# A second searched issue order for a fused attention and wave mixing kernel on one core

## The chip, the cores and the metric

The kernel runs on one core of a Trainium2 chip. The metric is device time in microseconds, the median of several executions; lower is better. TensorE (PE) multiplies matrices, VectorE (DVE), ScalarE (ACT) and GpSimd (POOL) work element by element, and SyncE (SP) only issues transfers. ACT and POOL issue transfers too. Each engine takes its own instructions strictly in the order in which they were written, and waits for the others by semaphores.

## The reference

Two blocks follow one another. All inputs are float32 in shape, with B = 4 batches, H = 4 heads, S = 1088 positions, D = 32 and R = 8.

```python
a = np.einsum('rd,bhsd->bhsr', S1, x)
b = np.einsum('rd,bhsd->bhsr', S2, x)
phi(x) = np.einsum('bhsi,bhsj->bhsij', a, b).reshape(..., 64)
...
kv = np.einsum('bhsf,bhsd->bhfd', phi(k), v)
z = np.sum(phi(k), axis=2)
num = np.einsum('bhsf,bhfd->bhsd', phi(q), kv)
den = np.einsum('bhsf,bhf->bhs', phi(q), z)[..., None] + 1e-06
x = (num / den), laid out as (4, 1088, 128)
...
theta = x @ w_theta
zr, zi = x * np.cos(theta), x * np.sin(theta)
y = einsum('ts,bsd->btd', w_tok_r, zr) + einsum('ts,bsd->btd', w_tok_i, zi)
u = x + y
return u + np.maximum(u @ w_ch, 0.0)
```

The two 1088 x 1088 token weights are the bulk of the arithmetic and of the loads. They arrive as 64-bit words and are decoded to float32 on the chip.

## The kernel before, in words

The kernel first writes its work down as a list of 1022 numbered operations (`Layout.op`), each with its engine (P for PE, V for DVE, A for ACT, G for POOL, S for SP), a function that issues its instructions, and the buffers that it reads and writes. The numbers follow the order of the program text. Then three tables decide the schedule, and nothing else does:

- `ORDER` holds the 1022 numbers in the order in which the operations are issued. An engine's own sequence is the part of `ORDER` that belongs to it, so moving a number moves the instructions and transfers of that operation past others on its queue.
- `PLACES` gives each of 419 buffers its slot in a pool: 22 slots of `big` (1152 words a partition), 5 of `zs`, one of `lv`, 6 of `hf`, 5 of `g3`, 6 of `g1`, 13 of `sm`, and 8 banks `ps` of the matmul accumulator. A buffer waits for the last reader of the buffer that had its slot.
- `SPINS` names operations ahead of which filler matmuls are issued ("70:2" is two ahead of operation 70). A filler (`spin`, L379) multiplies zeros, 128x384 in bf16, into a buffer that nothing reads. Ten more open the program and one stands after the first batch's scales.

In this order the operations' numbers are looked up when issued:

```python
self.order = [self.ops[int(i)] for i in ORDER.split()]
...
for o in self.order:
    n, home = spins.get(o.i, 0), None
    ...
    o.fn()
```

The stages of the work, batch by batch, are these.

- **Loads.** k, q and v of each batch are single transfers of 576 KB on SP (L614), batch 3's q four transfers (L609). w2 holds the two 128 x 128 weights of the second block. The token weights come in 17 rows of 1088 KB (L583, `zs` slots); ACT turns the two halves of each word into a float and a step (L584, L586), DVE shifts and adds them (L309 and the custom operation at L305).
- **Keys.** Transposes on PE, the features, and kv (`kfeatures`), the gram sums for the scales (`key_sums`), and a long chain of small DVE and PE operations that yields scales in powers of two (`chain`): once for batch 0, once for batch 1, and once for batches 2 and 3 together. The third starts with a sum over partitions: a DVE reduction (L849) and a matmul with ones (operation 281).
- **Queries.** Slices of q at fixed scale (`query_slices`), matmuls that give the feature sums at several precisions (`levels`, three PE operations a batch; ACT copies them out at L1002), and the denominator on DVE (L1003 to L1033, stage "den", which begins with the rounding that the profile shows as L309 `big<-lv`).
- **x, theta and z.** For each of three groups of columns: an outer product on DVE, its transposes (on PE for batches 0 and 1 at L1064, and for batches 2 and 3 by `turned`), the numerator on PE, theta on PE, two sines on ACT (L1114 to L1117 with the copies at L1111), and z = x cos, x sin on DVE (L305 `zs<-ps,g` or `zs<-g,g`).
- **turned** (L322): DVE transposes 32 x 32 blocks (L326); SP and ACT each scatter half of the result to DRAM in two transfers (L333, `fq` for outer products and `fx` for x); SP reads it back in the wanted layout (L338).
- **Mixing.** Batches 0 and 1 multiply each of the 17 z blocks by the matching weight row (`mix_row`), batch 0 for all three spans of columns (384, 384, 320) at once, batch 1 span by span. A float32 matmul shows as two records in the trace, so a row of batch 0 has six records and a step of batch 1 two. Batches 2 and 3 share seven products after Winograd (`winograd`), with sums of weight blocks on DVE (stage "ac").
- **Output.** The sum x + y, a matmul with w_ch, relu, sum and a transpose (`finish`, `finish_turned`), then stores of 32 columns each on SP and ACT (L1215).

The order of the stages in `ORDER` around the change: batch 1's mixing runs on PE while the queries of batches 2 and 3 go through DVE, ACT and the transfers. The first Winograd product follows as soon as batch 2's first z block is there.

Transfers issued by SP and ACT share a set of eight semaphores that are taken in turn, the "shared transfer queue of eight places": a transfer can be issued when the one eight before it has landed.

Of the kernel before, what the change touches and what calls it, by code (L numbers as in the profile page):

```python
# [76 lines left out]
)  # L77
SPINS = (
    "70:2 15:3 137:1 211:1 424:2 128:1 168:1 174:2 176:1 521:2 "
)  # L80
WARM = 0
SPLIT = ()
# [1330 lines left out]
```

## Time and profile before

| what | value |
|---|---|
| median of 3 runs | 219.65 us (219.24 to 219.75) |
| span of the profiled execution | 217.4 us |
| median less span | 2.25 us |
| instructions in the profile | 5063 |
| POOL and ACT, busy share | 10%, 51% |
| HBM read and written | 30.43 MB, 5.18 MB |

The profiled execution has no other time of its own than its span, which runs from its first to its last instruction. Times are microseconds. In the timeline views a row has the start, the duration, the engine, the source line, the operation, the tile that it writes, the tile that it reads, the shape, and how many alike follow one another; in brackets stands the idle time of the engine before it and what ended it. In the chain of waits a row has the start, the duration, the engine, the tile and the line. In the table of transfers the last column is the median time from issue to landing. An "x4" behind a matmul counts records.

### The profile page before, as it was taken

Reading aid. Unit: us, or ns where it says so; the run is one execution under the profiler, and the core shown is the slowest. Engines: PE = TensorE matmul, PEld = TensorE weight load, DVE = VectorE, ACT = ScalarE, POOL = GpSimd, SP = SyncE. Lnnn points to the kernel's source line nnn. Section 1 sums busy time; section 2 is a strip of 40 time slices with the busy share of each in tenths; the row PEclk is TensorE's granted clock in tenths of the full one; section 3 lists DMA queues with packets and bytes.
Section 4 is the critical chain, followed back from the end, with each engine's and each line's share of the span. In section 5 each row is a group of like instructions: output and inputs, shape, how many; then the busy total and the mean of one; then the engine's idle time right before and its main releaser. Section 6 shows DMA issues by size and latency. Waiting matters only on the chain.

```text
span 217.4 us, 5063 instructions
## 1 busy us (share of the span) xinstructions
PE 209.3 (96%) x1998; PEld 154.3 (71%) x1998; DVE 181.2 (83%) x408; ACT 111.2 (51%) x214; POOL 22.2 (10%) x44
## 2 busy tenths in 40 slices
PE   7999899999999999999999999999999999999994
PEld 3987786686766686666766575667758788888883
DVE  4899999999999999999599839988138999996542
ACT  3998498899779999983322040354037400000010
POOL 2237000055000000100132000100101000000000
PEclk9999999999999999999999999999999999999998
DMA  5999996869979979894226998599911000045253
GB/s 153 429 406 340 425 399 203 333 224 271 267 276 361 361 264 380 219 198 126 33 36 102 222 137 199 105 156 151 231 78 32 0 0 0 3 66 89 36 79 75
DMA packets 52635, 40.58 MB, mean 187 GB/s; under 512 B 45444, under 2 KB 47108, under 8 KB 50436
## 3 DMA queue, kind: packets, MB, share of 16 engines
q1 hardware_dynamic: 35540, 33.71, 48.7%
q0 software_dynamic: 1728, 4.65, 10.5%
q10 hardware_dynamic: 15344, 1.90, 6.0%
q8 instruction: 15, 0.25, 0.5%
q14 instruction: 8, 0.07, 0.1%
HBM read 30.43 MB, written 5.18 MB: 164 GB/s over the span
## 4 chain that ended last, share of the span: by engine, by line
PE 72%; DVE 12%; ACT 8%; DMA 4%; ACTq 2%; issue 2%; SPq 1%
PE ps L341 66%; DMA big<-q_l 2%; DVE lv L305 2%; PE ps L1064 2%; ACTq L333 2%; PE ps L1098 1%; DMA fx<-g 1%; DVE g L305 1%; DVE big L305 1%; PE ps L967 1%; ACT big L584 1%; ACT big L937 1%; DVE hf L309 1%; DVE zs L305 1%; ACT g L1068 1%
## 5 line engine op out<-in xcount | busy, mean ns | idle before, releaser
L341 PE MATMUL ps<-big,zs 128*128 128x384 f32 (+4 forms) x398 | 109.7, 424 | 0.4 <-DVE zs L305 0.4
L341 PEld LDWEIGHTS ps<-big,zs 128*128 128x128 f32 x398 | 71.4, 190 | 30.3 <-issue 2.6
L1201 ACT COPY g<-ps 128x128 f32<-128x128 f32 (+1 forms) x3 | 0.9, 301 | 42.5 <-PE ps L1193 42.5
L305 DVE CUSTOM_DVE_ANT_0 big<-big,big 128x2176 uint16<-128x2176 uint16 x17 | 21.8, 1287 | 0.4 <-ACT big L586 0.2
L584 ACT ACTIVATE big<-zs 128x1088 f32<-128x1088 f32 x17 | 20.9, 1235 | 2.1 <-DMA zs<-w_tok 1.2
L586 ACT ACTIVATE big<-zs 128x1088 int32<-128x1088 uint32 (+1 forms) x18 | 21.3, 1184 | 0.1
L341 PE MATMUL ps<-big,big 128*64 128x64 f32 (+2 forms) x208 | 20.6, 276 | 0.0
L341 PEld LDWEIGHTS ps<-big,big 128*64 128x64 f32 (+1 forms) x208 | 16.5, 154 | 2.9 <-issue 0.2
L305 DVE TENSOR_TENSOR big<-big,big 128x544 f32<-128x544 f32 x24 | 16.7, 712 | 0.0
L1002 ACT COPY lv<-ps 128x480 f32<-128x480 f32 x12 | 6.3, 563 | 14.2 <-PE ps L341 14.2
L312 DVE SCALAR_TENSOR_TENSOR g<-g,ps 128x384 f32<-128x384 f32 x12 | 6.6, 548 | 8.1 <-ACT g L1111 8.1
L1078 ACT COPY big<-ps 128x384 f32<-128x384 f32 x12 | 5.9, 489 | 14.0 <-PE ps L341 8.3
L309 DVE TENSOR_SCALAR big<-big 128x1088 int32<-128x1088 int32 x17 | 12.2, 724 | 0.6 <-ACT big L584 0.5
L341 PEld LDWEIGHTS ps<-w,big 128*128 128x128 f32 x80 | 10.6, 192 | 2.3 <-ACT g L1068 0.6
L319 POOL DMA_DIRECT2D big<-hf x6 | 5.4, 957 | 63.3 <-DVE g L312 33.8
L319 POOL DMA_DIRECT2D g<-big x6 | 5.2, 920 | 64.8 <-ACT g L1179 34.7
L341 PE MATMUL ps<-w,big 128*128 128x128 f32 x80 | 11.8, 280 | 0.0
L305 DVE TENSOR_TENSOR g<-lv 128x768 f32<-128x768 f32 x12 | 11.2, 945 | 0.0
L341 PE MATMUL ps<-g,sm 128*64 128x384 f32 x48 | 10.1, 507 | 0.2 <-ACT big L1078 0.2
L305 DVE TENSOR_TENSOR zs<-ps,g 128x768 f32<-128x768 f32 (+2 forms) x15 | 9.4, 632 | 1.0 <-PE ps L1098 0.9
L341 PEld LDWEIGHTS <-hf 128*64 128x64 f16 (+1 forms) x288 | 7.7, 110 | 2.9 <-issue 1.7
L379 PE MATMUL ps<-idle 128*128 128x384 bf16 x27 | 7.8, 400 | 1.3 <-POOL idle L381 1.3
(194 smaller groups left out, 336.6 us busy)
## 6 DMA issues: line engine op xcount, KB each, us to landing
zs<-w_tok SPq DMA_DIRECT2D x17, 1088.0 KB, 7.0
big<-k_l SPq DMA_DIRECT2D x6, 576.0 KB, 6.6
big<-hf POOLq DMA_DIRECT2D x6, 576.0 KB, 6.0
big<-v_l SPq DMA_DIRECT2D x4, 576.0 KB, 7.0
g<-fq SPq DMA_DIRECT2D x6, 384.0 KB, 5.2
big<-q_l SPq DMA_DIRECT2D x3, 576.0 KB, 5.1
fq<-g SPq DMA_DIRECT2D x12, 96.0 KB, 4.0
fq<-g ACTq DMA_DIRECT2D x12, 96.0 KB, 4.1
```

What stands on the lines that cost most here:

```text
L305: eng.tensor_tensor(out=o, in0=a, in1=b, op=f)
L309: (eng or V).tensor_scalar(out=o, in0=a, scalar1=s1, scalar2=s2, op0=op0, **kw)
L312: (eng or V).scalar_tensor_tensor(out=o, in0=a, scalar=s, in1=b, op0=op0, op1=op1)
L319: op("G", 0.9, lambda: G.dma_start(dst(), src(), accum_op=ALU.add), w, r, fly=fly)
L333: E.dma_start(there().rearrange("(a i) (x b j) -> b i x a j", a=nf, b=nf, j=SQ)[f], blocks()[f * SQ:(f + 1) * SQ].rearrange("i (x a j) -> ...
L341: T.matmul(o, lhs, rhs, start=start, stop=stop, skip_group_check=True)
L379: T.matmul(nowhere() if home is None else view(home, (GW,), F32), idle()[:, 0:P], idle(), start=True, stop=True, skip_group_check=True)
L584: op("A", 0.22 + n * 0.0009, lambda: A.activation(dfn(), words_of(raw(), n)[1].bitcast(F32), AF.Prelu, scale=2.0**-112, alpha=-(2.0**32)), ...
L586: op("A", 0.22 + n * 0.0009, lambda: A.activation(stp(), words_of(raw(), n)[0].bitcast(U32), AF.Copy, scale=2.0**-29), [stp], [raw])
L1002: op("A", act(480), lambda g=g, lp=lp: A.copy(lv().rearrange("p l (c n) -> p l c n", n=HR)[:, :, g * GC:(g + 1) * GC], lp().rearrange("p c ...
L1064: T.transpose(tr()[:, i * P:(i + 1) * P], qp()[:, i * H + 2 * n:i * H + 2 * n + 2].rearrange("p h i j -> p (h i j)"), ident())
L1078: op("A", act(GW), lambda g=g, xp=xp: A.copy(xt()[:, g * GW:(g + 1) * GW], xp()), cells(xt, g * GW, (g + 1) * GW), [xp])
```

## The change

Only the three tables are changed. No operation is added, removed or altered; the same 1022 numbers stand in `ORDER` in another sequence, so line numbers behind the tables fall by two. Positions that are the same on an engine's own list: 21 of 358 on PE, 33 of 347 on DVE, 27 of 214 on ACT, 8 of 38 on POOL, 17 of 66 on SP. 375 of the 419 places differ. There are 16 fillers by the old `SPINS` and 9 by the new, beside the ten and the one that stay.

```diff
 ORDER = (
-    "6 4 2 5 44 0 1 45 50 3 47 7 340 8 48 46 11 9 10 49 12 29 58 13 30 70 83 84 64 76 71 14 77 85 96 15 88 72 89 78 "
...
+    "6 4 0 5 44 1 58 47 45 7 50 8 340 9 49 10 11 2 48 12 29 355 84 83 70 30 76 13 46 71 64 85 14 59 86 88 77 15 61 87 60 "
...
 )
 SPINS = (
-    "70:2 15:3 137:1 211:1 424:2 128:1 168:1 174:2 176:1 521:2 "
+    "70:2 160:1 95:1 105:1 111:2 174:1 176:1 "
 )
```

Where the moved pieces that matter below stand, by operation number. Loads on SP, in their order:

```
before: s_t k0 q0 q1 k1 row1 k2 v0 k3 w2 row2 row5 row4 v1 ...
after:  s_t k0 w2 k1 q0 q1 row1 k3 k2 row4 v0 row2 v1 row0 row5 ...
```

Around operation 281 (batches 2 and 3's scale chain): operation 494 (a row of batch 0's mixing), 579 to 583 and 625 to 629 (steps of batch 1's mixing), 406 to 409 (row 14's decoding), 561 and 569 (phase multiplies) now stand ahead of it or of what it needs, and 571 (transposes) and 328 (a negation) no longer do.

Between batch 3's levels (719 to 724), its denominator (725 to 734) and the first product, the issue order is cut here to the operations concerned:

```
before: 719 721 720 723 722 724 725 675 726 504 727 728 729 686 688 682 687 676 735 736 689 839 691 838 702 695 787 796
after:  838 839 723 719 724 721 720 722 725 686 726 688 727 675 682 728 687 729 504 691 676 514 689 695 735 796 736 787 702
```

686 is the DVE transpose of `turned` for the first group of batch 2's x, 687 and 688 its scatters on SP and ACT, 689 its read-back, 675 and 682 read-backs of the outer products, 504 the four stores of batch 0's first span, 695 the z multiply that the first product needs, and 787 and 796 steps of that product. 735 and 736 (an outer product and its transpose), 838 and 839 (two weight sums), 702 (another transpose) and 514 (the last operation but one of batch 0's third span) are further DVE operations.

86 rows, old and new, of tables (ORDER, PLACES) are left out of this document.

## The prediction

> **What bounds the kernel now.** I read the span and the busy shares first, then the slices, to find where PE is not full.
>
> ```profile
> span 217.4 us, 5063 instructions
> PE 209.3 (96%) x1998; PEld 154.3 (71%) x1998; DVE 181.2 (83%) x408; ACT 111.2 (51%) x214; POOL 22.2 (10%) x44
> ...
> PE   7999899999999999999999999999999999999994
> ```
>
> PE is busy for 96% of the span: 8.1 us of idle time are all that is in sight. A busy PE need not be doing work, though, because matmuls are pipelined and a matmul that is held up counts as busy. So the next view is the windows, cut at 40 us and at two instructions that the rest of the argument needs. Columns: span, then busy us of PE, PEld, DVE, ACT and POOL, then granted clock, DMA share, GB/s.
>
> ```profile
> 0.00:40.00 40.00, 36.11 (x705) 29.01 (x706) 35.66 (x124) 31.76 (x73) 8.58 (x29) 1.00 0.86 330
> 40.00:90.90 50.90, 50.24 (x537) 35.34 (x536) 49.76 (x95) 46.84 (x81) 6.81 (x6) 1.00 0.89 297
> 90.90:145.10 54.20, 53.84 (x428) 34.50 (x426) 44.64 (x90) 19.20 (x34) 5.10 (x7) 1.00 0.69 136
> 145.10:214.00 68.90, 68.88 (x333) 55.49 (x333) 50.64 (x101) 13.10 (x28) 1.71 (x2) 1.00 0.35 66
> ```
>
> From 40 to 90.9 us three engines are full: DVE 49.76 of 50.90, PE 50.24, ACT 46.84. After 90.9 DVE has 9.6 us to spare and PE has 0.4, so there PE alone sets the time. Which engine sets it before 90.9 is told by PE's own groups in that stage (line, operation, count, busy us, mean ns), set against a later run of the same matmuls:
>
> ```profile
> L341 PE MATMUL ps<-big,zs 128*128 128x384 f32 x48 | 17.7, 492 | 0.0
> L341 PE MATMUL ps<-big,zs 128*128 128x320 f32 x24 | 8.4, 432 | 0.0
> ```
> ```profile
> 117.68 7.58 PE L341 MATMUL ps<-big,zs 128*128 128x320 f32 x24
> ```
>
> The mixing matmuls took 7.58/24 = 0.316 us a record there, including the drain of the last; I take 0.31. The 72 records of the stage should need 22.3 us and took 26.1: some 3.8 us of PE's "busy" time is waiting. DVE is therefore the limit up to 90.9 us, and PE after it. The place where one hands over to the other is the second-scale chain of batches 2 and 3:
>
> ```profile
> 85.72 0.45 DVE L309 TENSOR_SCALAR hf<-hf 128x1152 f16<-128x1152 f16 x1
> ...
> 90.25 0.22 DVE L849 TENSOR_REDUCE sm<-ps 128x8 f32<-128x64 f32 x1
> 90.38 0.95 DVE L305 TENSOR_TENSOR zs<-ps,g 128x768 f32<-128x768 f32 x1
> ...
> 91.52 0.73 DVE L309 TENSOR_SCALAR big<-big 128x1088 int32<-128x1088 int32 x1
> 92.38 1.29 DVE L305 CUSTOM_DVE_ANT_0 big<-big,big 128x2176 uint16<-128x2176 uint16 x1
> ```
> ```profile
> 90.92 0.28 PE L341 MATMUL ps<-sm,ones 128*128 128x8 f32 x2
> ```
>
> DVE's reduction at 90.25 feeds PE's matmul at 90.92 (op 281). PE takes its work in order, so what stands ahead of op 281 on PE is done while DVE is still the limit, and what stands behind it costs its full time.
>
> **The change, part by part.** No instruction changes, so the cost lies in which work falls on which side of such points. I took the sets ahead of op 281 in both orders, on PE directly, on the others by what op 281 needs.
>
> PE: newly ahead of it are one whole row of batch 0's mixing (op 494, 6 records) and five steps each of batch 1's first and third span (ops 579-583, 625-629, 20 records): 26 x 0.31 = 8.1 us. One group of three transposes (op 571) goes behind it.
>
> ```profile
> 72.57 0.33 PE ps L1098 x3
> ```
>
> That is 0.33, so 7.8 us of PE work leave the stretch that PE alone sets.
>
> DVE: newly ahead are the decoding of row 14 (0.73 + 1.29, the rows at 91.52 and 92.38) and two phase multiplies (0.95 each, the row at 90.38); gone is one negation (0.45). Batch 3's two outer products of about the same length change places. DVE's limit comes later by 2.02 + 1.90 - 0.45 = 3.5 us.
>
> Gross: 7.8 - 3.5 = 4.3 us earlier, if PE can do its added work in DVE's time. PE would need 50.24 - 3.8 + 7.8 = 54.2 us of the 50.9 + 3.5 = 54.4. It just fits; the rivals start from how closely.
>
> **Fillers.** Seven fewer, and all 16 and all 9 stand ahead of op 281. The ten that open the program stay.
>
> ```profile
> 1.34 3.38 PE L379 MATMUL ps<-idle 128*128 128x384 bf16 x10 [1.34 <-POOL idle L381]
> 4.69 0.49 PE L379 MATMUL ps<-idle 128*128 128x384 bf16 x2
> ...
> 6.44 0.65 PE L379 MATMUL ps<-idle 128*128 128x384 bf16 x3
> ```
>
> A third filler added 0.65 - 0.49 = 0.16 us. Seven are 1.1 us of PE time in a stretch that DVE sets, where DVE's work hides them: I count nothing. If PE set that stretch they would give 1.1 us; below nothing they can go only through the clock (a rival).
>
> The ten took 0.34 us each, over twice the later 0.16, and the granted clock is 1.00 in all four windows. By the Trainium skill ("TensorE: Matmul & The Clock Gate", Part 1: The HAM clock gate) TensorE starts at half clock, is raised after about 3.4 us of sustained work, and falls back after an idle window of about that length. The trace agrees with the start; by the rule fewer fillers could cost a second slow start, and by the trace, whose PE has no idle time of that length behind 2 us, they cost nothing.
>
> **Loads.** The new order issues w2 third instead of tenth, k1 ahead of q0, and row 5 much later.
>
> ```profile
> GB/s 153 429 406 340 425 399 203 333 224 271 267 276 361 361 264 380 219 198 126 33 36 102 222 137 199 105 156 151 231 78 32 0 0 0 3 66 89 36 79 75
> ...
> big<-k_l SPq DMA_DIRECT2D x6, 576.0 KB, 6.6
> ```
>
> At about 410 GB/s a load of 576 KB takes 1.4 us, which is what a swap by one place moves. DVE idles 4.3 of the first 40 us, so a better order of loads can give at most that, and one load that comes late costs 1.4. I take nothing, as DVE's work in that stretch is the same but for its order, and keep +1.4 and -3 (most of the idle time) for the range.
>
> **The hand-over to the products.** PE's stretch from 90.9 to 145.1 gets shorter only if the data for the Winograd products come earlier too. In the chain of waits:
>
> ```profile
> 83.10 44.99 PE ps L341 x362
> 128.11 0.57 ACT lv L1002
> ```
> ```profile
> 119.81 0.48 DVE L312 SCALAR_TENSOR_TENSOR g<-ps,g 128x320 f32<-128x320 f32 x1
> ...
> 128.70 0.46 DVE L309 TENSOR_SCALAR big<-lv 128x576 f32<-128x576 f32 x1 [4.64 <-ACT lv L1002]
> ...
> 132.13 0.57 DVE L326 STREAM_TRANSPOSE g<-big 128x384 f32<-128x384 f32 x1
> ...
> 136.57 0.92 DVE L305 TENSOR_TENSOR g<-lv 128x768 f32<-128x768 f32 x1
> 137.52 0.98 DVE L326 STREAM_TRANSPOSE g<-g 128x768 f32<-128x768 f32 x1
> 138.42 0.68 DVE L305 TENSOR_TENSOR big<-big,big 128x544 f32<-128x544 f32 x1
> ...
> 139.73 0.72 DVE L305 TENSOR_TENSOR big<-big,big 128x544 f32<-128x544 f32 x1
> ...
> 141.52 0.57 DVE L326 STREAM_TRANSPOSE g<-big 128x384 f32<-128x384 f32 x1
> ...
> 144.06 0.96 DVE L305 TENSOR_TENSOR zs<-g,g 128x768 f32<-128x768 f32 x1 [0.36 <-ACT g L1115]
> ```
> ```profile
> 145.07 1.19 PE L341 MATMUL ps<-big,zs 128*128 128x256 f32 x4 [0.36 <-DVE zs L305]
> ```
>
> PE's levels matmuls of batch 3 release the DVE chain at 128.70, and the first product follows 16.4 us later, with PE held up for 0.36. Between the last levels matmul and the first product the new order has six mixing steps and two product steps fewer and one output matmul more, two records each: 14 x 0.31 = 4.3 us less, so PE is ready 12.6 us after that matmul, against 17.0. On the chain, five DVE ops (136.57, 137.52, 138.42, 139.73, 141.52) leave, 0.92 + 0.98 + 0.68 + 0.72 + 0.57 = 3.9 us, and one of 0.48 (op 514, like 119.81) comes in: some 3.4 shorter, 13.0. From the matmul's end at 128.11 to the chain's start lie 0.59, so PE waits 0.59 + 13.0 - 12.6 = 1.0 instead of 0.36. The scatter with the read-back behind it gets its start 3.0 us sooner after the chain's first op, as the transposes (132.13) come right behind that op and four others behind them. Of the 0.64 I take half, 0.3, as ACT's part of the chain has fewer DVE results to wait for; both ends (0 and 0.64, and 4 where the chain isn't shortened) stay for the range.
>
> **Sum.** -7.8 + 3.5 + 0.3 = -4.0 us. The profiled 217.4 us become 213.4; the median of the runs, 219.65, lies 2.25 above the span, so 215.7.
>
> **The rivals.** First, the engines hold each other up.
>
> ```profile
> L1117 ACT ACTIVATE g<-g 128x384 f32<-128x384 f32 x5 | 2.6, 525 | 0.0
> ```
> ```profile
> L584 ACT ACTIVATE big<-zs 128x1088 f32<-128x1088 f32 x17 | 20.9, 1235 | 2.1 <-DMA zs<-w_tok 1.2
> ```
>
> Ahead of op 281 ACT gets row 14's two conversions (1.2 each) and four phase activations (0.53 each), 4.5 us more, so 51.3 of 54.4. With DVE at 53.3 and PE at 54.2, no engine can swallow another's wait. If half of the 3.8 us of PE's hidden waiting stays, the stage is 1.9 us longer: **217.6**. For it: all three are then above 94%. Against it: the same three were at 92 to 99% before, and DVE lost 1.1 us.
>
> Second, the clock falls back once: a second slow start costs 10 x (0.34 - 0.16) = 1.8 us: **217.5**. Against it stands the clock of 1.00.
>
> Third, the chain to the products isn't shortened (ACT or the transfers set it and not DVE). Of the 7.8 us moved, 4.3 are gone behind the levels matmuls and 3.5 ahead of them, where op 281 comes 3.5 later: the chain starts at 128.7 as before, and 16.4 us after it the product starts as before too. Nearly all is lost: **219.5**.
>
> Fourth, on the other side, the transfers of batch 2's turned x set the hand-over.
>
> ```profile
> 128.96 2.04 SPq L1215 DMA_DIRECT2D out<-g  x4
> ```
> ```profile
> g<-fq SPq DMA_DIRECT2D x6, 384.0 KB, 5.2
> ...
> fq<-g SPq DMA_DIRECT2D x12, 96.0 KB, 4.0
> ```
>
> The new order puts the four stores of out0_0 (op 504, 2.04 us of SP) between the scatter (op 687) and its read-back (op 689). With eight places in the shared queue a store waits for the landing of the eighth transfer before it, here a read-back of 5.2 us, and the read-back waits behind the store on SP. In series: transposes done at 129.7, scatter landed 4.0 later, stores 2.0, a landing of 5.2, the read-back's own 5.2 and the multiply of 1.0: the product starts at 147.1. It decides where the product starts later than 145.07; behind it PE has its 68.9 us in both orders, so the end is 2.0 later, **221.7**. Before, these stores stood ahead of the scatter. Against it: half of that series lay in parallel in the trace (the scatter and the landing overlap).
>
> **How the numbers follow.** Forecast 215.7, chance 0.56 (own range 214.0 to 217.0); engines 217.6, 0.18; clock 217.5, 0.04; chain not shortened 219.5, 0.08; transfers 221.7, 0.14. The range runs from 212.8 (the forecast with 3 us of the early idle time gone) to 219.9 (the third rival and 0.3, about what a measurement of this kernel tells from no change); outside are the fourth rival and a little below. Faster 0.56 + 0.18 + 0.04 = 0.78, same 0.08, slower 0.14.
>
> **What would show it.** Op 281 (L341, ps<-sm,ones, 128x8) should start at about 94.4 us with DVE as its releaser and almost no DVE idle between 40 and there; at 96 or later, the first rival holds. The first product (128x256, ps<-big,zs) should start near 141 with under 1 us of PE idle before it; near 145 it is the third rival, later the fourth, and SP's read-back of fx then stands behind the stores. PE's clock must stay 1.00 and fillers in the trace must be 0.16 apart behind the first ten. An idle time of DVE over 5 us in the first 40 would show the loads as the part I mis-sized.

## The result, and the profile after

The changed kernel is slower by 1.1%: a median of 222.29 us (222.21 to 222.66, 4 runs) against 219.70 us for the kernel before on the same chip (219.24 to 220.62, 4 runs), a ratio of 1.0109 [1.0066, 1.0153]. The forecast was 215.7 us, and its range ended at 219.9. The profiled execution spans 220.4 us, where the sum had 213.4: 7.0 us are to be found.

The page of the kernel after, in the same rows as before (busy share by engine; then the span in 40 slices of 5.5 us):

```profile
span 220.4 us, 5064 instructions
PE 209.3 (95%) x1991; PEld 157.9 (72%) x1991; DVE 182.5 (83%) x408; ACT 112.3 (51%) x215; POOL 20.4 (9%) x44
...
PE   6999959999899999999999998999989999999994
...
DVE  2899966998999999999689985999639899997342
...
PEclk9999996999999999999999999999999999999999
...
GB/s 173 429 414 411 424 410 418 375 229 110 107 300 407 318 196 164 347 107 89 128 106 3 73 234 103 222 146 174 200 234 36 12 48 36 30 1 11 1 66 74
```

PE is busy for the same 209.3 us as before, in a span 3.0 us longer. Its sixth slice is a 5 (27.6 to 33.1 us), where before no slice between the first and the last was below 8, and DVE's sixth and seventh slices are 6. ACT has 215 instructions instead of 214. The windows of the kernel after, at the cuts used for before (span, then busy us of PE, PEld, DVE, ACT, POOL, clock, DMA share, GB/s):

```profile
0.00:40.00 40.00, 35.09 (x654) 30.13 (x656) 29.82 (x110) 30.12 (x67) 8.85 (x30) 0.96 0.95 385
40.00:90.90 50.90, 49.98 (x502) 35.92 (x502) 49.51 (x101) 47.42 (x84) 4.03 (x5) 1.00 0.72 249
```

What is lost up to 90.9 us is lost in the first line: up to 40 us DVE does 29.82 us of work, where it did 35.66. It is 5.8 us behind there, while from 40 to 90.9 us it does nearly what it did before (49.51 against 49.76). The rows that the forecast named come out as follows, in PE's timeline of the kernel after:

```profile
100.02 0.39 PE L339 MATMUL ps<-sm,ones 128*128 128x8 f32 x2
...
146.93 5.52 PE L339 MATMUL ps<-big,zs 128*128 128x256 f32 x22
...
158.25 2.42 PE L339 MATMUL ps<-big,zs 128*128 128x256 f32 x10 [0.36 <-DVE zs L303]
...
164.20 0.87 PE L339 MATMUL ps<-g,sm 128*64 128x384 f32 x4 [0.95 <-DMA g<-fq]
```

Operation 281 starts at 100.02 us and not at 94.4: 5.6 us late. From it to the first product are 46.9 us, where the sum had 46.7. From the first product to the end of the span are 220.4 - 146.9 = 73.5 us, where before had 217.4 - 145.1 = 72.3: the two new waits in the last two rows, 1.3 us, explain the 1.2. So 5.6 + 0.2 + 1.2 = 7.0, and the question is what made operation 281 late.

DVE's waits in the first 40 us of the kernel after (what waited, for what, us in all, times, longest):

```profile
DVE sp L307 <- ACT sp L410: 3.1, 1, 3.1
DVE big L307 <- ACT lv L1000: 2.7, 1, 2.7
```

The first is at the start of the program; before, DVE went on at 3.25 us after a wait of 0.95. The second is the wait for batch 0's levels (queries), and behind it stands a stop of PE itself:

```profile
29.09 0.38 PE L339 MATMUL ps<-mv,hf 128*64 128x96 f16 x9
32.10 0.40 PE L339 MATMUL ps<-mv,hf 128*64 128x96 f16 x9 [2.63 <-issue]
```

PE stops for 2.63 us in the middle of a row of equal matmuls, and the releaser is "issue": no semaphore, no buffer and no other engine that the profile shows. Before has no such wait. Then the clock halves. A window of the kernel after behind the stop:

```profile
33.40:36.90 3.50, 3.50 (x70) 3.50 (x67) 2.21 (x6) 2.15 (x7) 0.00 (x0) 0.51 1.00 412
```

Three things are thus new in the first 40 us: a slow start, a stop of PE without a releaser, and some 3.4 us at half clock (0.51 over the window of 3.5).

### The profile page after: what moved, and what is told of

Same layout as the page of the kernel before. It is cut to its first block, busy times and chain, and to the rows that moved or that the text cites. A ratio compares the mean times of both kernels' runs of the same rounds, so it can differ in the third digit from the quotient of the medians.

```text
span 220.4 us, 5064 instructions
## 1 busy us (share of the span) xinstructions
PE 209.3 (95%) x1991; PEld 157.9 (72%) x1991; DVE 182.5 (83%) x408; ACT 112.3 (51%) x215; POOL 20.4 (9%) x44
## 4 chain that ended last, share of the span: by engine, by line
PE 56%; DVE 22%; DMA 12%; ACT 4%; issue 4%; ACTq 0%; SPq 0%; DVEq 0%
PE ps L339 48%; DVE big L303 8%; DMA fq<-g 6%; DMA g<-fq 4%; PE ps L737 2%; DVE g L324 2%; DVE g L303 2%; PE ps L1062 2%; DMA out<-g 2%; PE ps L965 2%; DVE lv L303 1%; DVE big L310 1%; DVE zs L303 1%; PE ps L1096 1%; DVE g L310 1%
## 5 line engine op out<-in xcount | busy, mean ns | idle before, releaser
L339 PE MATMUL ps<-big,big 128*64 128x64 f32 (+2 forms) x208 | 21.2, 282 | 0.0
L339 PEld LDWEIGHTS ps<-big,big 128*64 128x64 f32 (+1 forms) x208 | 17.0, 160 | 2.7
L1109 ACT ACTIVATE g<-ps 128x384 f32<-128x384 f32 x12 | 5.6, 484 | 10.8 <-DMA fq<-g 5.9
L339 PE MATMUL ps<-w,big 128*128 128x128 f32 x80 | 10.8, 276 | 0.0
L339 PE MATMUL ps<-mv,hf 128*64 128x96 f16 x216 | 7.1, 207 | 3.3 <-issue 2.6
L1112 ACT ACTIVATE g<-g 128x384 f32<-128x384 f32 x12 | 6.3, 523 | 5.2 <-DVE g L310 5.2
```

The source lines that it names most:

```text
L339: T.matmul(o, lhs, rhs, start=start, stop=stop, skip_group_check=True)
L1109: op("A", act(GW), lambda cs=cs, th=th: A.activation(cs()[:, 0], th(), AF.Copy, bias=ROUND), [(cs, 0)], [th])
L1112: op("A", act(GW), lambda cs=cs: A.activation(cs()[:, 0], cs()[:, 1], AF.Abs), [(cs, 0)], [(cs, 1)])
```

## The experiments

Three theories stand at the outset. **Constants:** operations 2 (DVE's constants, L357 to L371) and 3 (a first sine on ACT, which brings in the table of sines) stand at places 2 and 9 (counted from 0) of the order before and at 17 and 835 of the order after; that is the slow start. **Clock:** PE starts cold and falls back, and the slow matmuls make the rest late. **Fetch:** the stop is PE waiting for its own program, which comes over the same transfer engines as the loads. Its rival is that the stop belongs to the operation at which it stands. The expectations use letters: A is the constants, B that the loads in their new order come late and DVE waits for them, C the fetch, D that the stop belongs to its operation, E that short instructions outrun the fetch even without loads. Each run is compared with the kernel before on the same chip.

### Operations 2 and 3 early: e1_const_early and e1b_warm_early

```diff
-6 4 0 5 44 1 58 47 45
+6 4 2 0 5 44 1 58 3 47 45
...
-10 11 2 48 12
+10 11 48 12
...
-783 856 836 3 857
+783 856 836 857
```

> The changed kernel with two operations back at their earlier places: the constants (op 2, some 1.4 us of DVE memsets) ahead of the first weight unpacking, and the warming sine (op 3) behind it on ACT. Theory A (early stalls, one cause of which is where these two stand): DVE's first unpacking starts near 3.25 us and not 3.98, the first k sum near 5.4 and not 6.6, no second table load at 51.9, and PE doesn't idle 0.75 us ahead of its first transpose, so that the full clock is granted from about 4.7 us and not from 12.9: 1.5 to 3.5 us faster than the changed kernel, 219 to 220.8 us. Whether PE's stop of 2.6 us at 29.5 stays, theory A leaves open. Theory B (the loads in their new order are late and DVE waits for rows): within 0.3 us of 222.3.

Measured: 219.78 us against 219.77, ratio 1.0002 [0.9983, 1.0022], profiled span 218.5. Two moved numbers take back 2.5 us, the whole loss against before, as A had it; by B nothing should have changed. PE's timeline of this run:

```profile
30.75 0.43 PE L340 MATMUL ps<-mv,hf 128*64 128x96 f16 x9 [2.91 <-issue]
...
98.27 0.39 PE L340 MATMUL ps<-sm,ones 128*128 128x8 f32 x2
```

Operation 281 comes 1.75 us earlier, at 98.27, still 3.9 late. The stop is there as before, now of 2.91 us, though the operation is reached 1.6 us sooner.

The other run leaves the constants where they are, and moves operation 3 alone to right behind them:

```diff
-10 11 2 48 12
+10 11 2 3 48 12
...
-783 856 836 3 857
+783 856 836 857
```

> The changed kernel with only the warming sine (op 3) moved, to right behind the constants. Theory A: the table load of 1.3 us at 51.9 goes (DVE waits 0.7 and PE 0.9 us behind it there), and the start of the kernel stays as late as it is: 0.5 to 1.0 us faster, about 221.5 us. If the start is what counts and the table load is covered: within 0.3 of 222.3. Theory B: the same.

Measured: 221.76 us against 219.77, 1.0118 [1.0084, 1.0152], by the medians half a microsecond below the kernel after, with intervals that overlap. ACT's timeline tells what it changes. The kernel after:

```profile
2.41 1.28 ACT L410 ACT_TABLE_LOAD   x1 [2.41 <-DMA st<-s]
...
51.93 1.28 ACT L1115 ACT_TABLE_LOAD   x1
```

The table of sines is loaded at 51.93 us, in front of the first real sine, and that row stands on the chain of waits. In e1b it is loaded at 5.19 us, and in e1 one load at 1.59 us serves for all. The second load thus makes some 0.5 us of the loss, as far as four runs of each tell. The rest of the 2.5 is made at the start, in two ways that no run separates: the first table load begins at 2.41 us instead of 1.59, on the chain, and the late constants put 1.2 us of DVE's memsets (5.27 to 6.5 us) ahead of the first key sums, which come at 6.57 us; in e1 they come at 5.59 and in the order before at 5.39.

### The same the other way round: e4_before_late

```diff
-6 4 2 5 44 0 1 45 50 3 47 7
+6 4 5 44 0 1 45 50 47 7
...
-48 46 11 9 10
+48 46 11 2 9 10
...
-864 856 836 857
+864 856 836 3 857
```

> The kernel before with only the constants (op 2) and the warming sine (op 3) put as late as the changed kernel has them. Theory A: DVE starts 0.7 to 1.2 us later, a table load of 1.3 us comes in the middle, and if PE then idles before its first transpose the clock stays at half for longer: 1 to 3 us slower than the kernel before, 220.7 to 222.7 us. Theory B: within 0.3 of 219.7.

Measured: the order of before with both operations late takes 220.58 us against 219.77, 1.0048 [1.0033, 1.0063], slower by 0.8. The sign is as expected and the size is just below the range of 1 to 3 us; operation 281 moves from 90.92 to 92.14. The same two operations thus cost 2.5 us in one order and 0.8 in the other. Why the older order takes it better was not isolated.

### A warm clock: e2_clock_fillers

The kernel after with three more fillers where PE idles before full clock.

```diff
-70:2 160:1 95:1 105:1 111:2 174:1 176:1
+12:3 70:2 160:1 95:1 105:1 111:2 174:1 176:1
```

> The changed kernel with three more fillers ahead of PE's first transpose (op 12), so that PE doesn't idle from 4.7 to 5.5 us; the late constants stay. If the idle time is what keeps the clock at half until 12.9 us, full clock comes at about 4.7 to 6 us. Theory A holds DVE for the limit there, so little of it reaches the end: 0 to 1.0 us faster. If the slow clock itself is the cost: 2.5 to 4 us faster, 218.5 to 220.

Measured: 222.42 us against 219.77, 1.0142 [1.0105, 1.0179], no better than the kernel after. The mean granted clock of the profiled run is 1.000, against 0.992 for the kernel after, so the clock does not fall in this execution. (In two others of the four it was 0.992, and these took 222.18 and 221.78 us, no longer than the profiled one's 222.66.) From 4.7 to 13 us PE gets through 146 matmul records, where the kernel after has 77. But PE is stopped all the same:

```profile
31.41 0.45 PE L339 MATMUL ps<-mv,hf 128*64 128x96 f16 x12 [2.96 <-issue]
```

and two more stops without a releaser follow (5.4 us in all against 2.8). Operation 281 comes at 99.88, as in the kernel after. So a full clock from the first microseconds on, in that execution, brings nothing back: PE only arrives earlier at its stop.

### What the stop is: m3_short_alone and m4_short_loads

These two look at the stop by itself, and compute nothing of the reference: 700 equal short matmuls, with weights of 128x64, over 16 places of a bank, and the stores. m4 also issues the 17 loads of weight rows at the start; nothing reads them.

```diff
-LOADS = False
+LOADS = True
```

> Only 700 short float32 matmuls (64 columns out, 64 columns in, in turn to 16 places of one bank), about 2800 instructions of PE at some 50 a us, and zeros as output; all of the computation is left out. No loads. Theory C: no stop over 0.5 us. Rival E: stops at steps of 256 instructions also here.

> The same 700 short matmuls beside the 17 loads of weight rows (18.9 MB, some 45 us), which nothing reads; all of the computation is left out. Theory C: stops of 2 to 5 us at steps of 256 instructions while the loads run. Rival E: the same as without loads.

PE's timeline of m3, and of m4:

```profile
1.12 43.69 PE L63 MATMUL ps<-x,a 128*64 128x64 f32 x1400 [1.12 <-DVE x L54]
```
```profile
1.12 8.52 PE L63 MATMUL ps<-x,a 128*64 128x64 f32 x223 [1.12 <-DVE x L54]
11.60 5.50 PE L63 MATMUL ps<-x,a 128*64 128x64 f32 x128 [1.95 <-issue]
17.52 3.95 PE L63 MATMUL ps<-x,a 128*64 128x64 f32 x128 [0.43 <-issue]
23.44 3.95 PE L63 MATMUL ps<-x,a 128*64 128x64 f32 x128 [1.97 <-issue]
30.46 3.95 PE L63 MATMUL ps<-x,a 128*64 128x64 f32 x128 [3.07 <-issue]
36.93 3.95 PE L63 MATMUL ps<-x,a 128*64 128x64 f32 x128 [2.52 <-issue]
43.13 3.95 PE L63 MATMUL ps<-x,a 128*64 128x64 f32 x128 [2.25 <-issue]
49.05 13.67 PE L63 MATMUL ps<-x,a 128*64 128x64 f32 x409 [1.97 <-issue]
```

The executions took 57.73 and 75.68 us. Alone, the 1400 matmul records run through without a gap. Beside the loads the same instructions stop after every 128 matmul records, which with their weight loads are 256 instructions, for 14.2 us in all; when the loads are through, at about 48 us, there is no further stop in 409 records. The table of transfer queues on m4's page (packets, MB, share) has the carrier:

```profile
q8 instruction: 11, 0.18, 1.0%
```

0.18 MB in 11 packets are 16 KB each, and 2800 instructions of PE in blocks of 256 are 11 blocks. The operation at the stop plays no part, as all are equal. PE's program comes in 16 KB blocks over the transfer engines, and while these are full a block of 256 instructions takes 49.05 - 43.13 = 5.9 to 36.93 - 30.46 = 6.5 us, in one case 7.0. The two kernels of this study have 15 such packets each. The trace keeps the time of every packet, and this ties the two together: in m4 PE goes on 1.2 to 1.4 us after a packet of this queue has ended, at each of the seven stops. E falls with m3, which asks for as many instructions (2800 in 43.69 us, 64 a us) and never stops.

A first pair, m1_dense_alone and m2_dense_loads (700 matmuls 128x128 by 128x64 that add up in one place, without and with the same loads), gave 312.5 and 312.46 us and settled nothing: a record took 298.93/1400 = 0.21 us there, so that 256 instructions lasted 27 us and were never late.

> Only 700 matmuls of 128x128 by 128x64 in float32 on zeros, one after another (2800 instructions of PE in the trace), and zeros as output; all of the computation is left out. No loads. Theory C: no stop over 0.5 us. Rival E (the rate of short instructions alone outruns the fetch): stops about every 256 instructions, as with loads.

> The same 700 matmuls beside the 17 loads of weight rows (18.5 MB, some 45 us of transfers at 410 GB/s), which nothing reads; all of the computation is left out. Theory C: while the loads run PE stops for 2 to 4 us at steps of 256 instructions, and not behind them. Rival E: as without loads.

If the stop belongs to the program's fetch, it must fall at the same instruction whatever stands there. Windows from the start to the stop, of the kernel after, e1, e5 and e10 (the last two are told below):

```profile
0.00:29.47 29.47, 27.19 (x473) 22.66 (x473) 23.27 (x95) 23.75 (x54) 8.85 (x30) 1.00 0.93 372
```
```profile
0.00:30.70 30.70, 25.62 (x473) 20.34 (x473) 24.72 (x96) 24.47 (x56) 8.74 (x30) 1.00 0.93 371
```
```profile
0.00:30.20 30.20, 25.12 (x473) 19.92 (x473) 24.67 (x96) 24.18 (x56) 8.85 (x30) 1.00 0.93 369
```
```profile
0.00:29.90 29.90, 24.91 (x473) 20.03 (x474) 25.57 (x99) 24.45 (x55) 8.55 (x30) 1.00 0.92 367
```

473 matmul records each time (and in e11, told below), though PE gets there at 27.5 to 29.5 us, and though another operation stands there in e5 and e10 than in the others. The smaller stops of these and the other runs with this order stand at 346, 600 to 602 and 727 or 728 records: steps of 127, with their weight loads 254 instructions. The packet times agree: the third packet of the program ended at 30.81 us in the kernel after, 29.34 in e1, 28.90 in e5, 28.57 in e10 and 28.30 in e11, and PE goes on 1.3 to 1.4 us behind it in each. In the order before it ended at 26.93 us, and no stop follows. And the order after asks for more instructions there. Windows over the same 6.4 us, of the kernel after and of before:

```profile
23.10:29.50 6.40, 6.18 (x206) 5.70 (x205) 6.10 (x24) 6.40 (x12) 0.77 (x4) 1.00 1.00 414
```
```profile
23.10:29.50 6.40, 5.57 (x154) 4.96 (x154) 6.40 (x17) 3.83 (x7) 0.00 (x0) 1.00 1.02 420
```

411 instructions of PE against 308, at a DMA share of 1.00, where m4 needs (49.05 - 17.52)/5 = 6.3 us for a block of 256. The order before also drinks faster than that, but for less long: its loads ease off at 33 us (the seventh slice on its page has 203 GB/s), those of the order after hold 375 to 429 GB/s up to 44 us (its page, second to eighth slice).

### Another operation at the stop: e5, e6 and e8

If the stop sits at a fixed instruction, then moving work of PE behind the levels puts the levels ahead of it. e5 is e1 with operation 154 (the gram sums of batch 1's keys, for a later stage) moved behind the levels; e6 is the kernel after with the same move.

```diff
-347 121 154 212 122 124 123 214 420 236 230 153 82 424 346 422 145
+347 121 212 122 124 123 214 420 236 230 153 82 424 346 422 154 145
```

> The changed kernel with the constants and the warming sine early (as in the first experiment) and, besides, one PE operation moved: op 154 (36 trace instructions of key sums of batch 1) goes from ahead of batch 0's levels to right behind them (op 422). Theory C: PE's stop of 2.6 to 2.9 us, which fell on PE's instruction 961 in every kernel with this order, is a wait for PE's own program, fetched in blocks of 16 KB (256 instructions) behind the saturated loads. Then the stop stays at instruction 961, but the levels are complete by then, and DVE's wait of 3.5 us for their copies goes: 1.5 to 3 us faster than the first experiment's 219.8, 217 to 218.3. Rival D: the stop belongs to the third levels matmul, by an operand or a bank that the profile doesn't show: it goes where that matmul goes, and the time stays within 0.5 us of 219.8.

> The changed kernel with op 154 alone moved behind the levels of batch 0; constants and warming sine stay late. Theory C: DVE's wait of 2.7 us for the copies of the levels goes, the stop at instruction 961 stays: 1.5 to 3 us faster than the changed kernel, 219.3 to 220.8. Rival D: within 0.5 us of 222.3.

Both missed: 220.01 us against 219.74 for e5, 1.0019 [0.9994, 1.0043], and 222.36 for e6, 1.0112 [1.0073, 1.0151]. In e5 the stop is still in the levels:

```profile
30.23 0.30 PE L340 MATMUL ps<-mf,big 128*64 128x96 f32 x2 [2.04 <-issue]
```

Three records of the levels were left behind it (the row shows two of them), so DVE waits 2.2 us for them instead of 3.5; and at the next two blocks PE stops for 1.4 and 1.1 us, where e1 had no stop and 0.7. Operation 281 comes at 97.72, 0.55 earlier than in e1. The move bore out where the stop sits, and showed that the next blocks are late too.

e8 takes five fillers out of e5, to bring the levels ahead of the stop.

```diff
-70:2 160:1 95:1 105:1 111:2 174:1 176:1
+70:2 174:1 176:1
```

> The kernel of the fifth experiment (constants early, op 154 behind the levels) without five fillers that stood ahead of the levels, ten trace instructions. There the stop at instruction 961 fell three records short of the levels' end. Theory C: the levels now end ahead of the stop, DVE's wait of 2.2 us for their copies goes, and the time falls by 0.5 to 2 us to 218 to 219.5; were the fetch not what stops PE, five empty matmuls less would change nothing (within 0.4 us of 220.0).

Measured: 221.18 us against 219.61, 1.0057 [1.0038, 1.0076], a miss. The stop is behind the levels, but operation 281 comes at 97.67, hardly earlier than in e5 (97.72): DVE waits for the sums that PE computes next instead.

```profile
34.14 0.29 DVE L304 TENSOR_TENSOR sm<-ps,sm 128x128 f32<-128x128 f32 x1 [2.95 <-PE ps L340]
```

What makes it slower than e5 stands at the hand-over. DVE's wait from 97 to 148 us, and PE's first product:

```profile
DVE g L325 <- DMA out<-g: 2.1, 1, 2.1
```
```profile
147.09 1.10 PE L340 MATMUL ps<-big,zs 128*128 128x256 f32 x4 [1.86 <-DVE zs L304]
```

DVE waits for stores of finished output to land before it may write their buffer again, and PE waits for DVE. This is the fourth rival in part: the stores land late and set the hand-over, but what waits for them is DVE's next transpose, by its buffer, and not the read-back on SP.

### Key features later: e9 and e10

e9 is e1 with batch 3's key transposes and features (operations 227 to 242 and 253) moved from before 30 us to about 50, with new slots. e10 moves only 229, 235 and 241 with their copies, to just behind the levels.

```diff
-198 119 241 120
+198 119 120
...
-365 425 155 348 423 242 426
+365 425 155 235 229 348 423 236 426 230 336 156 241
```

> The first experiment's kernel with batch 3's key features moved from the stretch at 18 to 41 us to about 46 to 55 us, where the earlier order had them from 30 us on: 90 trace instructions of PE (9 transposes and 36 feature matmuls) and six copies on ACT, with the join that follows them, in other slots. Theory C (PE's program arrives at 256 instructions in some 6.3 us there): the levels of batch 0 end at about instruction 886, ahead of the stop at 961; all that follows stands 90 instructions earlier in the program, worth 90 / 256 x 6.3 = 2.2 us up to 47 us. DVE's wait of 3.5 us for the levels falls under 1 us; the sum-of-scales matmul (128x8) starts at 95.5 to 97 us and not 98.3; the time is 1 to 2.5 us below the first experiment's 219.8, 217.3 to 218.8. If the fetch isn't what limits, moving work from an early to a later stretch, where DVE and ACT are full, makes it no faster or slower: 219.8 to 221.

> The first experiment's kernel with only batch 3's 36 feature matmuls and their three copies (72 trace instructions of PE) moved, from right ahead of the levels of batch 0 to some 4 us behind them; the transposes stay. Theory C: the levels end at about instruction 904, ahead of the stop at 961, which stays; DVE's wait of 3.5 us for the levels' copies falls under 1 us; as PE's program still comes at 256 instructions in 6.3 us up to 47 us, only a part of that reaches the scales matmul (98.3): by 50 us DVE has done 1 to 1.5 us more, and the time is 0.5 to 1.5 us below 219.8, 218.3 to 219.3. If the levels' wait isn't what sets it, within 0.4 us of 219.8.

e9 takes 222.81 us against 219.43, 1.0152 [1.012, 1.0183], a miss: the moved work cost more at its new place. Windows of e9 and e1 there:

```profile
50.00:60.00 10.00, 9.23 (x115) 7.06 (x110) 7.20 (x14) 8.89 (x19) 2.54 (x3) 1.00 0.30 73
```
```profile
50.00:60.00 10.00, 10.00 (x124) 7.51 (x120) 9.93 (x18) 9.73 (x17) 1.42 (x2) 1.00 0.44 103
```

DVE loses 2.7 us there, waiting for batch 1's levels (2.2 us). e10 takes 220.00 us against 219.45, 1.0011 [0.9983, 1.0039]. DVE's wait for the levels is gone, but it waits 2.1 us for PE's sums behind the stop instead; operation 281 comes at 97.14, 1.1 earlier than in e1, and the first product starts at 145.73, with PE held up for 0.81; e1 has it at 145.06. The expected 0.5 to 1.5 us did not come: another miss. In e5, e8, e9 and e10 alike, whatever stood behind the block's end was late.

### Fewer loads: e7, e11 and e12

The other way to test the fetch is to free the transfer engines. e7 is e1 without the loads of seven weight rows, which are decoded from row 4's words instead; e11 leaves out four loads of q, k and v as well and takes batch 0's in their place; e12 is the order before with six weight rows and the same four loads left out, as the control for what lighter loads give any order. The instructions on the engines are the same.

```diff
+SAMEL = (('v', 1), ('q', 1), ('q', 2), ('k', 1))
...
+if (nm, b) in SAMEL:
+    t = ld[nm, b] = ld[nm, 0]
+    op("S", 0.0, lambda: None, [], [])
+    return
```

> The changed kernel with constants and warming sine early, and with the loads of seven weight rows (0, 2, 3, 5, 6, 8, 10) left out: these rows are decoded from row 4's words, so the token weights are wrong; every instruction of PE, DVE and ACT stays. Theory C (PE's program is fetched behind saturated loads): with the loads done by about 25 us the blocks of PE's program come within 1 to 2 us, PE's stops without a releaser go (2.9 and 0.7 us in the first experiment), and so do DVE's wait of 3.5 us for the levels and the second slow stretch of the clock; the sum-of-scales matmul (128x8) starts at 93 to 96 us and not 98.3, and the time is 2 to 5 us below the first experiment's 219.8. Rival E (the rate of short instructions outruns the fetch whatever the loads do): the stop at instruction 961 stays at 2 us or more and the time within 1 us.

> The first experiment's kernel with most early loads left out: seven weight rows are decoded from row 4's words, and batch 1's k, q and v and batch 2's q are batch 0's, so the output is wrong; every instruction of PE, DVE and ACT stays in its order. The loads that are left should be done by some 20 us. Theory C: the blocks of PE's program come within 2 us of need, no stop without a releaser over 0.5 us is left from 20 to 50 us, the scales matmul (128x8) starts at 94 to 96.5 us (94.4 was the forecast for the changed kernel) and not 98.3, and the time is 215.5 to 218. If DVE's and ACT's order is late in itself: 97.5 or later, and 219 or more.

> The kernel before with about the same early loads left out (six weight rows decoded from row 1's or row 4's words, batch 1's k, q and v and batch 2's q from batch 0's; the output is wrong, every instruction of PE, DVE and ACT stays). Theory C: it had no stop of PE without a releaser, so it gains little: 0 to 1 us, 218.7 to 219.7. If lighter loads speed every order alike, it gains as much as the other kernel of this pair.

Measured: e7 218.95 us against 219.61, 0.9967 [0.9937, 0.9996]; e11 218.53 against 219.80, 0.9927 [0.9895, 0.996]; e12 219.02 against 219.80, 0.9968 [0.9948, 0.9989]. e7 missed its range (214.8 to 217.8) by 1.2 us, and by its own sign spoke for E: the stop stays (2.74 us). But the rows that were left out come late in the queue, so the loads still fill the engines to 33 us, and it decides nothing. In e11 they ease off at 27 us, and this is PE's timeline:

```profile
29.64 0.40 PE L341 MATMUL ps<-mv,hf 128*64 128x96 f16 x9 [2.11 <-issue]
...
95.36 0.39 PE L341 MATMUL ps<-sm,ones 128*128 128x8 f32 x2
...
143.42 5.52 PE L341 MATMUL ps<-big,zs 128*128 128x256 f32 x22
```

Operation 281 comes at 95.36, 2.9 us sooner than in e1 and 1.0 us from the forecast's 94.4. In e12 it moves by 0.6 us, from 90.92 to 90.36. So by one profile of each, lighter loads give the new order 2.9 us at operation 281 and the old one 0.6.

The 2.9 us are not the price of the stop, though. e11 was expected to have no stop over 0.5 us, and it has one of 2.11, 0.8 shorter than e1's, as the packet begins only at 27.20 us, when the loads ease off. Two other things change with it: e1's second stop (0.66) is gone, and the clock stays at 1.00 behind the stop, where it fell to half in e1. In DVE's work the gain lies where these are: from 27 to 38 us DVE does 8.58 us of work in e11 and 6.70 in e1, 1.9 us more.

Of the 2.9 only 1.3 us reach the end, and e11 misses its range (215.5 to 218) too. From operation 281 to the first product e1 takes 145.06 - 98.27 = 46.8 us and e11 143.42 - 95.36 = 48.1. The chain of waits shows what lies there. The kernel after, from the last DVE transpose of an outer product on:

```profile
128.41 4.30 DMA fq<-g
...
132.72 3.95 DMA fq<-g
...
137.11 4.03 DMA g<-fq
...
141.15 2.24 DMA out<-g
...
145.94 0.85 DVE zs L303
```

Two scatters, a read-back and the landing of a store follow one another, 15 us of transfers in series, and then the multiply that the first product needs. The same rows in e11:

```profile
123.75 4.39 DMA fq<-g
...
128.15 4.59 DMA fq<-g
...
133.27 4.41 DMA g<-fq
...
137.70 2.22 DMA out<-g
```

There they take 4.39 + 4.59 + 4.41 + 2.22 = 15.6 us, in e1 4.14 + 4.12 + 4.07 + 1.99 = 14.3: the 1.3 us that e11 loses between operation 281 and the product. Why each transfer is slower in e11 was not isolated.

## Why the prediction was wrong, point by point

**The loads step failed.** It was the only term for the first 40 us but the fillers, and stood at nothing. It read: "I take nothing, as DVE's work in that stretch is the same but for its order". DVE does not get through the same work up to 40 us: 29.82 us against 35.66. The forecast named the sign that would tell so, over 5 us of idle time in DVE's first 40, and there were 10.2. The step looked at bytes per second and at which load changes places with which, and the loads themselves did keep DVE supplied (none of its waits over 0.2 us there in the kernel after is for a load). Two things that it did not look at make up most of the gap of 5.6 us at operation 281:

- The **constants and the first sine** were moved late. This was in the order of operations and could have been read there: the first DVE rows (memsets from 5.27 us on, ahead of the first key sums at 6.57) and an ACT table load of 1.28 us on the chain. Moved back (e1), 1.75 us at operation 281 and 2.5 us in the median; in the old order (e4) the same two cost 0.8 us.
- **PE's program arrives late**, as the new order asks for 411 PE instructions in 6.4 us while the loads fill the transfer engines. That this is the stop is shown by m3 and m4, by the count of 473 in five kernels and by the packet times. Its price is not: lighter loads gave 2.9 us at operation 281 (the control 0.6), with a shorter stop, one stop less and a clock that did not fall. The rival, that the stop belongs to its operation, falls with m4, where all operations are equal.

1.75 + 2.9 leave 1.0 us of the 5.6, which no run places. At the end of the program e11 gains 0.73% and the control 0.32%, with intervals that overlap, so how much of the final time the fetch costs stays open between nothing and some 1.3 us.

**DVE as the limit up to operation 281, PE behind it**: right. From 40 to 90.9 us DVE is busy for 49.51 of 50.90, and the 5.8 us that it is behind at 40 us are there again at operation 281, as 5.6.

**7.8 us of PE work moved ahead, the hand-over at 46.7 us behind operation 281**: right in size, 46.9. In its cause the step was half right. PE has its work without idle time, as forecast, but the chain beside it is no longer DVE's: it runs through 15 us of transfers. The **fourth rival** gave 0.14 to transfers that set the product. Its late stores are there, with another wait behind them than the one it named, and level with PE: with a small push (e8) it sets the first product and costs 1.9 us of PE time, and it takes 1.3 us from e11. By an estimate from these, even with operation 281 at 94.4, at e1's 46.8 to e11's 48.1 us the product would have come at 141.2 to 142.5, and with 73.5 us behind it the span would have been 214.7 to 216.0: 1.4 to 2.7 us gained, not 4.

**From the first product on**: the sum took 72.3 us in both orders, and it is 73.5, from two waits (0.95 for batch 3's read-back, 0.36 for a multiply). This term, 1.2 us, was missing.

**The fillers**: no run prices them alone. e8 has five fewer and e2 three more, and in both other things move with them.

**The clock** (second rival, 0.04): the mechanism came, and the price did not. PE's timeline of the kernel after:

```profile
5.47 0.37 PE L434 MATMUL ps<-ident,m 128*2 128x128 f32 x1 [0.75 <-DVE m L453]
...
11.73 1.44 PE L339 MATMUL ps<-sbk,g 128*64 128x64 f32 x24
...
20.50 0.92 PE L339 MATMUL ps<-sbk,g 128*64 128x64 f32 x24
```

Behind the opening fillers PE idles for 0.75 us, and 24 records that take 0.92 us later still take 1.44 at 11.73; after the stop of 2.63 us the clock is at 0.51 for 3.5 us. By the Trainium skill ("TensorE: Matmul & The Clock Gate", Part 1: The HAM clock gate) full clock takes about 3.4 us of sustained work, and an idle window of that length takes it away; windows run freely. The half clock lasted some 3.4 us, as that rule has it, but an idle time of 2.63 us was enough here, while 2.04 us in e5, and 2.96 in e2, left the clock at 1.00. The traces show what tells them apart: the granted clock changes in steps of 3.413 us, and counted by these steps every step with 1.95 us of idle PE or more was followed by half clock (the stop of the kernel after has 2.09 us in one step, e1's 2.91), and none with 1.76 or less (e5's has 1.60, and e2's falls into two steps, 1.57 and 1.39). Between them stand one step of 1.91 that kept the clock (e8) and one of 1.77 that lost it (e10, at the end of the kernel). The forecast's sentence that fewer fillers cost nothing "by the trace" relied on PE having no long idle time; the new order made one. Yet e2, with the clock at 1.00 from 6 us on in its profile, is no faster, so PE's clock was not what counted there.

**The first rival** (engines hold each other up, 0.18) would by its own sign hold, as operation 281 is behind 96 us; but its place, 40 to 90.9 us, lost only 0.25 us of DVE's time. It was not the cause. **The third** (the chain isn't shortened) falls: the stretch shrank from 54.2 to 46.9 us.

Two ends of the forecast's range are a tenth off by its own terms (215.7 - 3 = 212.7 and 219.5 + 0.3 = 219.8); nothing hangs on that.

Of the versions run, none that does all the work beats the kernel before: e1, e5 and e10 lie within their intervals of it.

## What to carry to other kernels

When an order is changed, read the first microseconds by operation, not by bytes: what the start-up operations (constants, first use of a table) stand behind is paid by everything after them when the limiting engine has no slack. Count TensorE's instructions per microsecond while loads saturate the transfer engines: many short matmuls there can run ahead of their own program, which shows as idle time released by "issue". And before a gain in the early stage is booked, follow the next hand-over's chain through its transfers, because a chain of equal length beside PE keeps what the early stage gains.

## What the runs showed of the hardware

- TensorE's program is transferred while it runs, in 16 KB packets of 256 instructions, and beside the data these come late: with 415 GB/s of loads a block took 5.9 to 7.0 us and PE stopped for 0.4 to 3.1 us per block (m4); with idle transfer engines the same 1400 records ran without a gap (43.69 us, m3). PE went on 1.2 to 1.4 us after a packet had ended. The Trainium skill ("Trainium Architecture — The Big Picture", The software stack) has each engine's instruction stream copied into the engine's memory when the program is loaded. In these executions that sentence is not the whole of it: 11 to 15 packets of the queue "instruction" moved while they ran.
- float32 matmuls 128x128 by 128x64 that add up in one place took 0.21 us a record (m1); such over 16 places, half as many columns of weights, took 0.031 us (m3).
- The clock is granted in steps of 3.413 us. A step in which PE was idle for 1.95 us or more was followed by half clock, one with 1.76 us or less was not, whatever the length of the idle time as a whole (2.96 us over two steps in e2 kept it).
